# Softmax attention and a slot mixture of experts on one core: late weights, the last values' place, and the merge of the last slots

## The chip, the cores and the metric

The kernel runs on one core of a Trainium2 chip. Its time is the device time of one execution in microseconds (us). Before the change three runs took 321.18, 322.11 and 323.55 us; the median is 322.11.

## The reference

Attention over 8 batches, 12 heads, 448 rows and 64 columns, whose softmax has exp(-m) added to its denominator, and then a mixture of experts with slots: 3584 rows of 768, 32 slots, 8 experts of 4 slots, hidden size 1024.

```python
scores = scale * np.matmul(q, k.transpose(0, 1, 3, 2))
m = np.max(scores, axis=-1, keepdims=True)
e = np.exp(scores - m)
attn = e / (np.sum(e, axis=-1, keepdims=True) + np.exp(-m) + 1e-09)
x = np.matmul(attn, v)                 # laid out as (3584, 768)

logits = x @ phi                       # (3584, 32)
d = np.exp(logits - logits.max(0, keepdims=True))
d /= d.sum(0, keepdims=True) + 1e-09
slot_input = (d.T @ x).reshape(8, 4, 768)
for e in range(8):
    slot_out[e] = np.maximum(slot_input[e] @ w1[e], 0.0) @ w2[e]
c = np.exp(logits - logits.max(1, keepdims=True))
c /= c.sum(1, keepdims=True) + 1e-09
out = c @ slot_out.reshape(32, 768)
```

All inputs and the output are float32; the kernel loads q, k and the weights as bf16 (the DMA converts them) and v as float32.

## The kernel before

**Units and steps.** The attention is cut into 24 units, each of two batches and two heads. A unit has 7 tiles of rows, and the main loop takes one tile per step `n`, so that unit `u` begins at step 7u and the score loop ends at `end` = 168. A plan written by hand, `at(n, where, f)`, sets what else is done at which step and in which place of it: small, av, value, rooms, end, load, in an order that the loop at line 800 shows. Each engine works through its own instructions in the order of the program; nothing is reordered.

**A unit's stages.** `stage_T` transposes q and k on TensorE (L241). `stage_S` forms the scores, and VectorE takes their row maxima (L264). `stage_MT` transposes the maxima (L272), copies them (`mt`, L276) and GpSimd builds from them the matrix `md` (L282, L288). `stage_ST`, ten steps behind the scores, puts -m into PSUM with a matmul by `md` (L300), adds the scores (L305), and ScalarE takes exp (L309). `stage_V` casts v to bf16 on GpSimd (L314). `stage_AV` multiplies (L336), `stage_AVout` copies the product out of PSUM (L347, L350), `stage_den` adds exp(-m) to the sums on GpSimd (L356), and `stage_N` divides (L362, L364). `stage_X` transposes the result for the logits (L419, L420). The last unit, 23, goes another way: `last_sinks` puts exp(-m) in order (L376, L378), and `stage_last` adds, inverts and multiplies straight from PSUM (L387 to L399).

**Mixture.** After every six units, `mixture` forms logits, running maxima and sums, and the slots' input. The last of the four calls does this along `slot_max`, `slot_exp`, `slots_T`, `slot_in` (14 matmuls, L519), `merge` (which weighs the four partial sums by partition block, L626 to L630) and `experts_in`: VectorE adds the new product to the accumulated slots (`ld`, L674), twelve matmuls bring them across partitions (L678), two matmuls give the denominators (L671), and L682, L683 and L685 divide. `gate_logits` in between transposes the logits for the gate (L576). Then come the first expert product (L705), the relu, the second expert product (`outer`, L824) in two halves of columns and two groups of experts, and the output: 28 row tiles, each of two matmuls (L884; the first ones L849 and L881), a copy by VectorE or ScalarE, and a DMA from SyncE's queue (L854, L889).

**Weights.** Each weight load is half an expert matrix: 768 KB as bf16, 1.5 MB in DRAM. 24 of them lie in `wres`, fetched throughout the score loop (L180). The eight others, rooms 0 to 7, are halves of the second matrices of experts 4 to 7. They lie in `block`, where q, k, v, the exponentials and x are until the attention has read them. So their loads come late and in pieces, at the steps that the table at line 789 lists; rooms 6 and 7 follow `slot_in`, which has to read x first. These loads are issued by GpSimd, between its own operations and in order with them; v's loads are issued by SyncE. Each load waits until the former contents of its place have been read.

**Places.** x has seven places in `block`, `x0` and six others in a row; unit u takes place (u + 4) mod 7. The raw values of the last unit lie, before the change, where q and k of that unit were (`qr` and `kr`), which are columns of room 1.

```python
for n, i, js in ((end - 5, 0, (3, 1)), (end - 5, 1, (0, 1)), (end - 2, 1, (1, 3)), (end + 2, 2, (0, 2)),
                 (end + 4, 3, (0, 1)), (end + 4, 2, (2, 2)), (end + 7, 3, (1, 2)), (end + 9, 3, (3, 1)), (end + 9, 4, (0, 3)),
                 (end + 12, 4, (3, 1)), (end + 12, 5, (0, 3)), (end + 18, 5, (3, 1))):
    at(n, "load", lambda i=i, js=js: load_w(WRES + i, *js))
```

Of the kernel before, what the change touches and what calls it, by code (L numbers as in the profile page):

```python
# [20 lines left out]
WRES = 24  # L21
# [3 lines left out]
def kernel(  # L25
# [75 lines left out]
    def xbuf(u):  # L101
        return block[:, ds(xbuf_at((u + 4) % (HP + 1)), N2)]

    def xruns(u):

        runs = []
        for i in range(HP):
            at_ = (u + i + 4) % (HP + 1)
            if runs and at_ > 1 and i % 4:
                runs[-1][1] += 1  # L110
            else:
                runs.append([i, 1, xbuf_at(at_)])
        return [(i, k, block[:, ds(o, k * N2)].rearrange("p (i s n) -> p i s n", i=k, s=TB))
                for i, k, o in runs]
# [40 lines left out]
        RAW[0, "qr"] = t_  # L155

    def load_v(u):
        t_ = block[:, ds(parts["vr" if u < U - 1 else "qr"][0], 2 * N2)].bitcast(F32).rearrange("p (h n) -> p h n", h=2)
        RAW[u, "vr"] = load(u, t_, v, nc.sync if u else nc.gpsimd)

    W = {}
# [5 lines left out]
    def load_w(i, j0=0, m=None, p0=0, rows=128):  # L167


        kind, e, half = weights[i]  # L170
        if kind == 1:
            J, n = KC // 2, F
            src = moe_w1[e].rearrange("(p j) f -> p j f", p=128)[:, ds(half * J, J), :]
        else:
            J, n = FK // 2, DD
            src = moe_w2[e, ds(half * 128 * J, 128 * J)].rearrange("(p j) f -> p j f", p=128)
        js = ds(2 * j0, 2 * (m or J))
        t_ = room(i, n // 2)
        src = src.rearrange("p j (h n) -> p (j h) n", h=2)
        gdma(out=t_[ds(p0, rows), js, :], in_=src[ds(p0, rows), js, :])  # L180
        for j in range(j0, j0 + (m or J)):
            W[kind, e, half * J + j] = t_[:, ds(2 * j, 2), :]
# [187 lines left out]

    def last_sinks(u):
        em = EM.pop(u)
        ems = small.tile([128, 2, TB], F32, tag="den", name="den").rearrange("p b g -> p (b g)")
        DEN[u] = ems
        for b in range(2):
            nc.gpsimd.tensor_copy(  # L376
                ems[:, ts(b, 2 * C3)].rearrange("p (h c) -> p h c", h=2), em[:, :, ds(b * C3, C3)])
        nc.gpsimd.tensor_copy(ems[:, ds(4 * C3, 2)], em[:, :, TB - 1])  # L378

    def stage_last(u):  # L380
        av = AV.pop(u)
        ems = DEN.pop(u)
        drec = small.tile([128, 2, TB], F32, tag="rec", name="rec", bufs=1).rearrange("p b g -> p (b g)")
        x = xbuf(u).rearrange("p (s n) -> p s n", s=TB)
        main = av[:, :, ds(0, 2 * C3 * 65)].rearrange("p b (g e) -> p b g e", e=65)
        rest = av[:, :, ds(2 * C3 * 65, 65)]
        nc.vector.scalar_tensor_tensor(  # L387
            drec[:, ds(0, 4 * C3)].rearrange("p (b g) -> p b g", b=2), main[:, :, :, D], 1e-9,
            ems[:, ds(0, 4 * C3)].rearrange("p (b g) -> p b g", b=2), op0=ALU.add, op1=ALU.add)
        nc.vector.scalar_tensor_tensor(drec[:, ds(4 * C3, 2)], rest[:, :, D], 1e-9,  # L390
                                       ems[:, ds(4 * C3, 2)], op0=ALU.add, op1=ALU.add)
        nc.vector.reciprocal(drec, drec)
        for b in range(2):
            nc.vector.tensor_tensor(
                x[:, ds(b * C3, C3), :].rearrange("p c (h d) -> p h c d", h=2),
                main[:, b].rearrange("p (h c) e -> p h c e", h=2)[:, :, :, ds(0, D)],
                drec[:, ts(b, 2 * C3)].rearrange("p (h c) -> p h c", h=2).unsqueeze(3)
                    .broadcast_to([128, 2, C3, D]), op=ALU.mult)
        nc.vector.tensor_tensor(  # L399
            x[:, TB - 1, :].rearrange("p (h d) -> p h d", h=2), rest[:, :, ds(0, D)],  # L400
            drec[:, ds(4 * C3, 2)].unsqueeze(2).broadcast_to([128, 2, D]), op=ALU.mult)
        X[u] = x


# [27 lines left out]
    def mixture(bp, n, at):  # L432
# [78 lines left out]

        def slot_in():

            ps = slot([128, DD])
            for s, (i, k, x) in ([(s, r) for r in xruns(bp * HP) for s in range(TB)] if final else
                                 [(s, r) for s in range(TB) for r in xruns(bp * HP)]):
                    b, c = divmod(s, C3) if s < 2 * C3 else (0, C3)
                    cs = ds(32 * c, 32)
                    nc.tensor.matmul(ps[cs, ds(i * 128, k * 128)], d_sb[:, b, cs], x[:, :, s, :],  # L519
                                     start=(b == 0 and i % 4 == 0), stop=(b == 1 or c == C3),  # L520
                                     tile_position=(0, 32 * c), skip_group_check=True)
            for i in range(HP):
                X.pop(bp * HP + i)
            if first:
                nc.vector.tensor_copy(acc, ps)
            elif not final:
                rescale(acc, alpha, ps)
            else:
                last_state["ps"] = ps

        if final:
            at(n - 28, "end", lambda: logits((0, 1)))
            at(n - 2, "end", lambda: logits((2, 3, 4), close=False))
            at(n, "end", lambda: logits((5,)))
            at(n, "end", lambda: gate_logits(0))
            at(n, "end", lambda: warm(1))
            at(n + 2, "small", slot_max)
            at(n + 3, "small", slot_exp)
            at(n + 3, "small", lambda: last_state["lT"]())
            at(n + 4, "end", slots_T)  # L540
            at(n + 4, "end", lambda: last_state["gl"][0]())
            at(n + 4, "end", lambda: warm(1))
            at(n, "load", lambda: nc.gpsimd.memset(SI, 0.0))
            at(n + 5, "small", slot_sum)
            at(n + 7, "end", slot_in)
            at(n + 7, "end", lambda: [load_w(WRES + i) for i in (6, 7)])
            at(n + 7, "end", lambda: gate_logits(1))
            at(n + 7, "end", lambda: last_state["gl"][1]())
            at(n + 7, "end", experts_in)
            at(n + 7, "end", experts_hidden)  # L550
        else:
            for j in range(0, HP, 2):
                at(n - 7 * (HP - 2 - j), "end", lambda j=j: logits((j, j + 1)))
# [68 lines left out]
    def merge():  # L622


        for i in range(4):
            nc.vector.tensor_copy(wcol[ds(32 * i, 32), :], ef[:, ds(i, 1)])  # L626
        nc.vector.tensor_scalar(rden, fold, wcol, None, op0=ALU.mult)
# [39 lines left out]

    def experts_in():

        den = slot([128, NS])  # L670
        nc.tensor.matmul(den, sums, rden, start=True, stop=True)  # L671
        si = ld.rearrange("s (p j) -> s j p", j=KC)
        ps = spare(ds(0, KC * NS)).rearrange("p (j n) -> p j n", j=KC)
        nc.vector.scalar_tensor_tensor(ld, acc, last_state["alpha"], last_state["ps"],  # L674
                                       op0=ALU.mult, op1=ALU.add)
        for j in range(KC):
            for i in range(2):
                nc.tensor.matmul(ps[:, j, :], si[:, j, :], fw[:, i, :], start=(i == 0), stop=(i == 1))  # L678
# [68 lines left out]
    def at(n, where, f):  # L747
        plan.setdefault((n, where), []).append(f)

    for u in range(U):  # L750
# [64 lines left out]

    os_ = [slot([128, 384]) for half in range(2)]

    def outer(half, jh, gs):
        J = FK // 2
        for g in gs:  # L820
            for j in range(J):
                for e in range(4):
                    es = ds(32 * e, 32)
                    nc.tensor.matmul(os_[half][es, :], HT[jh][:, g, j, es],  # L824
# [35 lines left out]
    outer(0, 1, (0,))  # L860
    outer(1, 1, (0,))
    first_weights()
    outer(0, 1, (1,))
    nc.scalar.copy(so[:, 0, :], os_[0])
    outer(1, 1, (1,))
    nc.vector.tensor_copy(so[:, 1, :], os_[1])
    first_tiles(0, nc.scalar.copy)
    first_tiles(1, nc.vector.tensor_copy)
# [51 lines left out]
```

## Time and profile before

| | |
|---|---|
| median of three runs | 322.11 us (321.18 to 323.55) |
| profiled execution, own time | 319.92 us |
| its span, first to last instruction | 318.1 us |
| TensorE matmul busy | 277.0 us (87%) |
| VectorE, ScalarE, GpSimd busy | 253.6, 211.7, 229.1 us |
| read from and written to HBM | 83.46 MB, 11.01 MB |
| mean granted TensorE clock | 0.96 |

The profile is of one execution. PE is a matmul on TensorE, PEld a weight load there, DVE is VectorE, ACT ScalarE, POOL GpSimd, SP SyncE. A row of the timeline gives start, duration, engine, line, operation, out<-in, count and, in brackets, how long the engine was idle before it and what ended that. A row of the windows gives for a stretch the busy time of each engine, then the granted TensorE clock, the busy share of the 16 DMA engines and the GB/s that they moved. Where a load converts float32 to bf16, those are the bytes written.

### The profile page before, as it was taken

How to read it: one execution, taken by the hardware profiler on the slowest of the kernel's cores; microseconds unless marked ns; L12 is line 12 of the kernel's file. 1: busy time of each engine (PE TensorE's matmuls, PEld its weight loads, DVE VectorE, ACT ScalarE, POOL GpSimd, SP SyncE). 2: the span in 40 equal slices, each digit the busy share in tenths (PEclk: the TensorE clock that was granted, in tenths of full speed). 3: DMA queues.
4: the chain of work that ended last, by engine and by line, in shares of the span. 5: the costliest groups of instructions: out<-in, count | busy, mean ns of one | idle time of the engine just before them, and what ended most of it. 6: DMA issues, size and time to landing. Idle time of an engine off the chain costs nothing.

```text
span 318.1 us, 13342 instructions
## 1 busy us (share of the span) xinstructions
PE 277.0 (87%) x5861; PEld 159.1 (50%) x5862; DVE 253.6 (80%) x340; ACT 211.7 (67%) x338; POOL 229.1 (72%) x337
## 2 busy tenths in 40 slices
PE   1669989999899899999999999999999988986910
PEld 1325655465555465655655665555556545542300
DVE  2988988898799799999999999999999736527720
ACT  3026867777687677787877788777878885237610
POOL 7476798789898688899898889889984876620000
PEclk9999999999999999999999999999999999998555
DMA  7979999999999979999999999999999799958997
GB/s 131 172 94 187 178 169 190 172 169 183 184 184 192 158 118 174 176 182 145 195 170 184 149 155 202 179 153 154 181 184 195 123 156 202 214 119 305 396 400 287
DMA packets 49130, 59.34 MB, mean 187 GB/s; under 512 B 4560, under 2 KB 44496, under 8 KB 49072
## 3 DMA queue, kind: packets, MB, share of 16 engines
q0 software_dynamic: 37856, 36.46, 76.0%
q1 hardware_dynamic: 11216, 22.03, 20.9%
q8 instruction: 46, 0.75, 0.9%
q14 instruction: 12, 0.10, 0.1%
HBM read 83.46 MB, written 11.01 MB: 297 GB/s over the span
## 4 chain that ended last, share of the span: by engine, by line
PE 67%; DVE 11%; DMA 5%; POOL 5%; issue 4%; ACT 3%; SPq 0%; POOLq 0%; ACTq 0%; DVEq 0%
PE av L336 16%; PE ps L256 12%; PE ps L300 12%; PE ps L305 9%; PE ps L241 6%; DMA block<-in_moe_w_dram 4%; PE ps L419 3%; DVE block L264 3%; PE ps L884 3%; ACT block L309 2%; DVE m L264 2%; PE ps L260 2%; PE av L272 1%; POOL block L282 1%; DMA wres<-in_q_dram 1%
## 5 line engine op out<-in xcount | busy, mean ns | idle before, releaser
L309 ACT ACTIVATE block<-ps 128x896 bf16<-128x896 f32 x168 | 153.8, 917 | 56.0 <-PE ps L305 53.4
L264 DVE TENSOR_REDUCE block<-ps 128x2 bf16<-128x896 f32 x84 | 90.8, 1090 | 15.4 <-PE ps L256 13.8
L264 DVE TENSOR_REDUCE m<-ps 128x2 bf16<-128x896 f32 x84 | 90.8, 1090 | 4.7 <-PE ps L256 3.2
L336 PE MATMUL av<-block 64*128 64x65 bf16 (+1 forms) x2688 | 90.1, 193 | 3.1 <-issue 1.9
L336 PEld LDWEIGHTS <-block 64*128 64x128 bf16 (+1 forms) x2688 | 75.5, 97 | 32.5 <-issue 10.5
L300 PE MATMUL ps<-block,ones 64*64 64x448 bf16 x672 | 69.7, 368 | 4.5 <-POOL block L288 1.4
L305 PE MATMUL ps<-block 64*64 64x448 bf16 x672 | 66.4, 353 | 1.3 <-issue 1.3
L256 PE MATMUL ps<-block 64*128 64x448 bf16 x288 | 54.1, 372 | 3.3 <-DVE m L264 1.3
L256 PEld LDWEIGHTS <-block 64*128 64x128 bf16 x288 | 19.8, 94 | 52.6 <-issue 48.0
L282 POOL TENSOR_TENSOR block<-mt,nmask 128x768 bf16<-128x768 bf16 x24 | 35.2, 1468 | 12.7 <-ACT mt L276 11.6
L136 POOL DMA_DIRECT2D block<-in_q_dram x46 | 27.4, 602 | 18.7 <-PE ps L241 17.3
L364 POOL TENSOR_TENSOR block<-block,rec 128x896 bf16<-128x896 f32 x22 | 37.5, 1704 | 0.5
L180 POOL DMA_DIRECT2D wres<-in_moe_w_dram x48 | 35.0, 731 | 1.4
L300 PEld LDWEIGHTS <-ones 64*64 64x64 bf16 x672 | 24.7, 105 | 9.2 <-issue 4.1
L136 POOL DMA_DIRECT2D block<-in_k_dram x46 | 27.8, 622 | 1.2 <-ACT block L309 1.2
L244 DVE COPY block<-ps 128x896 bf16<-128x896 bf16 x48 | 27.8, 615 | 0.5 <-PE ps L241 0.3
L305 PEld LDWEIGHTS <-block 64*64 64x64 bf16 x672 | 24.5, 107 | 1.8 <-issue 1.7
L241 PE MATMUL ps<-ident,block 128*64 128x128 bf16 x644 | 24.6, 229 | 0.9 <-issue 0.4
L241 PEld LDWEIGHTS <-block 128*64 128x64 bf16 x644 | 20.4, 115 | 4.1 <-issue 2.0
L314 POOL CAST block<-block 128x896 bf16<-128x896 f32 x24 | 22.5, 937 | 0.0
L347 ACT COPY block<-av 128x780 f32<-128x780 f32 x22 | 17.7, 804 | 0.1
L420 DVE COPY block<-ps 128x896 bf16<-128x896 bf16 (+1 forms) x23 | 14.0, 607 | 1.8 <-PE ps L419 1.8
(161 smaller groups left out, 250.3 us busy)
## 6 DMA issues: line engine op xcount, KB each, us to landing
wres<-in_moe_w_dram POOLq DMA_DIRECT2D x48, 384.0 KB, 5.7
out_dram<-wres SPq DMA_DIRECT2D x27, 384.0 KB, 4.5
block<-in_v_dram SPq DMA_DIRECT2D x46, 224.0 KB, 6.2
block<-in_q_dram POOLq DMA_DIRECT2D x46, 112.0 KB, 6.2
block<-in_k_dram POOLq DMA_DIRECT2D x46, 112.0 KB, 6.2
block<-in_moe_w_dram POOLq DMA_DIRECT2D x4, 576.0 KB, 7.6
block<-in_moe_w_dram POOLq DMA_DIRECT2D x2, 768.0 KB, 11.4
block<-in_moe_w_dram POOLq DMA_DIRECT2D x6, 192.0 KB, 6.0
```

The source lines that it names most:

```text
L136: eng.dma_start(out=t_[ds(b * P, P), :, :], in_=src[bp * 2 + b, ds(hp * 2, 2)].rearrange("h (p t) d -> p h (t d)", t=TB))
L180: gdma(out=t_[ds(p0, rows), js, :], in_=src[ds(p0, rows), js, :])
L241: nc.tensor.transpose(ps[ds(h * D, D), :, ds(t * P, P)], r[:, h, ds(t * D, D)], ident)
L244: nc.vector.tensor_copy(t_, ps)
L256: nc.tensor.matmul(ps[:, h, ds(0, S)], QT[u][hs, b, ds(c * 128, 128)], KT[u][hs, b, :], start=True, stop=True)
L264: nc.vector.tensor_reduce(m[:, :, s], ps[:, :, ds(0, S)], axis=AX.X, op=ALU.max)
L282: nc.gpsimd.tensor_tensor(md[:, :, ds(0, C3 * 128)].rearrange("p b (e n) -> p b e n", n=P), mt.unsqueeze(1).unsqueeze(1).broadcast_to([128 ...
L300: nc.tensor.matmul(ps[ds(b * P, P), h, ds(0, S)], ones[hs, :], MD[u][hs, b, :], start=True, stop=False)
L305: nc.tensor.matmul(ps[ds(b * P, P), h, ds(0, S)], KT[u][hs, b, ds(t * P, P)], QT[u][hs, b, :], start=False, stop=True)
L309: nc.scalar.activation(et, ps[:, :, ds(0, S)], AF.Exp, scale=scale)
L336: nc.tensor.matmul(o, et[bs, h, ds(c * 128, w)], V65[u][bs, h, t, ds(0, 65)], start=(t == 0 and h == 0 and c == 0), stop=(t == TB - 1), sk ...
L364: (nc.gpsimd if u < U - 2 else nc.vector).tensor_tensor(x.rearrange("p s (h d) -> p h s d", h=2), xv[:, :, :, ds(0, D)], rec.unsqueeze(3). ...
```

## The change

It has eight parts.

- The raw values of the last unit go to the places of x of units 22 and 23, which are free from the former mixture until those units' x is written.
- The room that this frees in `qr` and `kr` takes two of room 1's four pieces (384 KB), loaded at step `end` - 9; the other two follow at `end` - 5. There is no load at `end` - 2 any more.
- `stage_den` of unit 21 is one step later, so that on GpSimd the last unit's `md` comes ahead of it.
- The load of room 7 is split into a load of three pieces and one of one piece, and the last group of `outer` does the first three pieces for both halves of columns and then the last piece for both. The cast of the first half follows both halves' matmuls in the program.
- `slot_in` of the last mixture writes two tiles of 384 columns in place of one of 768, and `experts_in` merges and multiplies by halves; the denominators' matmuls come between the halves. So that a half of the slots' columns is a set of whole products, the first expert matrix is laid out by contiguous halves.
- `merge` broadcasts the running sum on GpSimd, ahead of its two casts, and no longer on VectorE.
- `stage_last` adds the 14 sums in one instruction; `last_sinks` orders them to fit.
- `xruns` of the last mixture makes runs of three units in place of four and two; the number of matmuls stays 14.

On each engine the order of all other instructions is the same. GpSimd has two instructions more (a load and the broadcast), VectorE one fewer.

```diff
-    def xruns(u):
+    def xruns(u, most=4):
...
-            if runs and at_ > 1 and i % 4:
+            if runs and at_ > 1 and i % most:
...
-        t_ = block[:, ds(parts["vr" if u < U - 1 else "qr"][0], 2 * N2)]...
+        t_ = block[:, ds(parts["vr"][0] if u < U - 1 else xbuf_at((U - 2 + 4) % (HP + 1)), 2 * N2)]...
...
-            src = moe_w1[e].rearrange("(p j) f -> p j f", p=128)[:, ds(half * J, J), :]
+            src = moe_w1[e, ds(half * 128 * J, 128 * J)].rearrange("(p j) f -> p j f", p=128)
...
     def stage_last(u):
...
-        nc.vector.scalar_tensor_tensor(
-            drec[:, ds(0, 4 * C3)].rearrange("p (b g) -> p b g", b=2), main[:, :, :, D], 1e-9,
-            ems[:, ds(0, 4 * C3)].rearrange("p (b g) -> p b g", b=2), op0=ALU.add, op1=ALU.add)
-        nc.vector.scalar_tensor_tensor(drec[:, ds(4 * C3, 2)], rest[:, :, D], 1e-9,
-                                       ems[:, ds(4 * C3, 2)], op0=ALU.add, op1=ALU.add)
+        both = av[:, :, ds(0, TB * 65)].rearrange("p b (g e) -> p b g e", e=65)
+        nc.vector.scalar_tensor_tensor(drec, both[:, :, :, D], 1e-9, ems, op0=ALU.add, op1=ALU.add)
...
-            ps = slot([128, DD])
-            for s, (i, k, x) in ([(s, r) for r in xruns(bp * HP) for s in range(TB)] if final else
+            pss = [slot([128, DD // 2]) for _ in range(2)] if final else [slot([128, DD])]
+            for s, (i, k, x) in ([(s, r) for r in xruns(bp * HP, 3) for s in range(TB)] if final else
                                  [(s, r) for s in range(TB) for r in xruns(bp * HP)]):
+                    ps, i = (pss[i // 3], i % 3) if final else (pss[0], i)
...
-            at(n + 7, "end", lambda: [load_w(WRES + i) for i in (6, 7)])
+            at(n + 7, "end", lambda: [load_w(WRES + 6), load_w(WRES + 7, 0, 3), load_w(WRES + 7, 3, 1)])
...
     def merge():
+        nc.gpsimd.tensor_copy(sums, srun.broadcast_to([128, 128]))
         for i in range(4):
             nc.vector.tensor_copy(wcol[ds(32 * i, 32), :], ef[:, ds(i, 1)])
         nc.vector.tensor_scalar(rden, fold, wcol, None, op0=ALU.mult)
         nc.gpsimd.tensor_copy(fw[:, 0, :], rden)
         nc.gpsimd.tensor_tensor(fw[:, 1, :], rden, fw[:, 0, :], op=ALU.subtract)
-        nc.vector.tensor_copy(sums, srun.broadcast_to([128, 128]))
...
     def experts_in():
-        den = slot([128, NS])
-        nc.tensor.matmul(den, sums, rden, start=True, stop=True)
-        si = ld.rearrange("s (p j) -> s j p", j=KC)
+        si = ld.rearrange("s (a p j) -> s a j p", a=2, j=KC // 2)
         ps = spare(ds(0, KC * NS)).rearrange("p (j n) -> p j n", j=KC)
-        nc.vector.scalar_tensor_tensor(ld, acc, last_state["alpha"], last_state["ps"],
-                                       op0=ALU.mult, op1=ALU.add)
-        for j in range(KC):
-            for i in range(2):
-                nc.tensor.matmul(ps[:, j, :], si[:, j, :], fw[:, i, :], start=(i == 0), stop=(i == 1))
+        for a, half in enumerate(last_state["ps"]):
+            cs = ts(a, DD // 2)
+            nc.vector.scalar_tensor_tensor(ld[:, cs], acc[:, cs], last_state["alpha"], half,
+                                           op0=ALU.mult, op1=ALU.add)
+            for j in range(a * KC // 2, (a + 1) * KC // 2):
+                for i in range(2):
+                    nc.tensor.matmul(ps[:, j, :], si[:, a, j % (KC // 2), :], fw[:, i, :], start=(i == 0), stop=(i == 1))
+            if a == 0:
+                den = slot([128, NS])
+                nc.tensor.matmul(den, sums, rden, start=True, stop=True)
...
-            at(n + 20, "value", lambda u=u: stage_den(u))
+            at(n + (20 if u != U - 3 else 21), "value", lambda u=u: stage_den(u))
...
-    for n, i, js in ((end - 5, 0, (3, 1)), (end - 5, 1, (0, 1)), (end - 2, 1, (1, 3)), (end + 2, 2, (0, 2)),
+    for n, i, js in ((end - 9, 1, (2, 2)), (end - 5, 0, (3, 1)), (end - 5, 1, (0, 2)), (end + 2, 2, (0, 2)),
...
-    def outer(half, jh, gs):
+    def outer(half, jh, gs, js=range(FK // 2)):
...
-            for j in range(J):
+            for j in js:
...
     first_weights()
-    outer(0, 1, (1,))
+    for js in (range(3), (3,)):
+        for half in range(2):
+            outer(half, 1, (1,), js)
     nc.scalar.copy(so[:, 0, :], os_[0])
-    outer(1, 1, (1,))
     nc.vector.tensor_copy(so[:, 1, :], os_[1])
```

More of the change, by code (lines that the diff above doesn't have):

```diff
@@ L157, in load_v @@
     def load_v(u):
-        t_ = block[:, ds(parts["vr" if u < U - 1 else "qr"][0], 2 * N2)].bitcast(F32).rearrange("p (h n) -> p h n", h=2)
+        t_ = block[:, ds(parts["vr"][0] if u < U - 1 else xbuf_at((U - 2 + 4) % (HP + 1)), 2 * N2)].bitcast(F32).rearrange("p (h n) -> p h n", h=2)
         RAW[u, "vr"] = load(u, t_, v, nc.sync if u else nc.gpsimd)
@@ L372, in last_sinks @@
         em = EM.pop(u)
-        ems = small.tile([128, 2, TB], F32, tag="den", name="den").rearrange("p b g -> p (b g)")
+        ems = small.tile([128, 2, TB], F32, tag="den", name="den")
         DEN[u] = ems
@@ L376, in last_sinks @@
             nc.gpsimd.tensor_copy(
-                ems[:, ts(b, 2 * C3)].rearrange("p (h c) -> p h c", h=2), em[:, :, ds(b * C3, C3)])
-        nc.gpsimd.tensor_copy(ems[:, ds(4 * C3, 2)], em[:, :, TB - 1])
+                ems[:, b, ds(0, 2 * C3)].rearrange("p (h c) -> p h c", h=2), em[:, :, ds(b * C3, C3)])
+        nc.gpsimd.tensor_copy(ems[:, :, TB - 1], em[:, :, TB - 1])
     def stage_last(u):
@@ L382, in stage_last @@
         ems = DEN.pop(u)
-        drec = small.tile([128, 2, TB], F32, tag="rec", name="rec", bufs=1).rearrange("p b g -> p (b g)")
+        drec = small.tile([128, 2, TB], F32, tag="rec", name="rec", bufs=1)
         x = xbuf(u).rearrange("p (s n) -> p s n", s=TB)
-        main = av[:, :, ds(0, 2 * C3 * 65)].rearrange("p b (g e) -> p b g e", e=65)
-        rest = av[:, :, ds(2 * C3 * 65, 65)]
-        nc.vector.scalar_tensor_tensor(
-            drec[:, ds(0, 4 * C3)].rearrange("p (b g) -> p b g", b=2), main[:, :, :, D], 1e-9,
-            ems[:, ds(0, 4 * C3)].rearrange("p (b g) -> p b g", b=2), op0=ALU.add, op1=ALU.add)
-        nc.vector.scalar_tensor_tensor(drec[:, ds(4 * C3, 2)], rest[:, :, D], 1e-9,
-                                       ems[:, ds(4 * C3, 2)], op0=ALU.add, op1=ALU.add)
+        both = av[:, :, ds(0, TB * 65)].rearrange("p b (g e) -> p b g e", e=65)
+        nc.vector.scalar_tensor_tensor(drec, both[:, :, :, D], 1e-9, ems, op0=ALU.add, op1=ALU.add)
         nc.vector.reciprocal(drec, drec)
@@ L395, in stage_last @@
                 x[:, ds(b * C3, C3), :].rearrange("p c (h d) -> p h c d", h=2),
-                main[:, b].rearrange("p (h c) e -> p h c e", h=2)[:, :, :, ds(0, D)],
-                drec[:, ts(b, 2 * C3)].rearrange("p (h c) -> p h c", h=2).unsqueeze(3)
+                both[:, b, ds(0, 2 * C3)].rearrange("p (h c) e -> p h c e", h=2)[:, :, :, ds(0, D)],
+                drec[:, b, ds(0, 2 * C3)].rearrange("p (h c) -> p h c", h=2).unsqueeze(3)
                     .broadcast_to([128, 2, C3, D]), op=ALU.mult)
         nc.vector.tensor_tensor(
-            x[:, TB - 1, :].rearrange("p (h d) -> p h d", h=2), rest[:, :, ds(0, D)],
-            drec[:, ds(4 * C3, 2)].unsqueeze(2).broadcast_to([128, 2, D]), op=ALU.mult)
+            x[:, TB - 1, :].rearrange("p (h d) -> p h d", h=2), both[:, :, TB - 1, ds(0, D)],
+            drec[:, :, TB - 1].unsqueeze(2).broadcast_to([128, 2, D]), op=ALU.mult)
         X[u] = x
@@ L524, in slot_in @@
             if first:
-                nc.vector.tensor_copy(acc, ps)
+                nc.vector.tensor_copy(acc, pss[0])
             elif not final:
-                rescale(acc, alpha, ps)
+                rescale(acc, alpha, pss[0])
             else:
-                last_state["ps"] = ps
+                last_state["ps"] = pss
         if final:
```

## Prediction

> **What bounds the kernel now.** I read the page's chain first, then the windows of the last 75 us with their DMA columns, then the timeline of each engine around every edited line. Line numbers are those of the kernel before. The chain in order of time (start, us, what):
>
> ```profile
> 255.70 0.36 POOL block L288
> ...
> 256.11 0.38 PE ps L300 x4
> ...
> 271.52 12.92 DMA block<-in_moe_w_dram
> ...
> 284.48 1.47 PE ps L824 x29
> ...
> 285.98 0.57 DVE wres L866
> ...
> 287.11 0.97 DVE wres L853
> ```
>
> Three things set the end. The last unit's bias matrix on GpSimd lets the scores of L300 start; much later the last weight load lets the last 29 matmuls of L824 start; after them two casts and two copies release the output. The windows say what the DMA engines do meanwhile (last columns: granted clock, DMA share, GB/s written):
>
> ```profile
> 247.00:249.50 2.50, 2.47 (x62) 1.26 (x56) 2.31 (x4) 1.83 (x2) 1.87 (x2) 1.00 0.34 44
> ...
> 258.00:259.60 1.60, 0.85 (x23) 0.40 (x16) 1.26 (x2) 1.60 (x3) 1.43 (x8) 1.00 0.73 90
> 259.60:264.50 4.90, 4.90 (x150) 3.32 (x148) 1.96 (x3) 4.03 (x5) 2.73 (x6) 1.00 1.03 173
> 264.50:283.10 18.60, 16.50 (x275) 9.26 (x274) 10.74 (x38) 6.47 (x17) 10.57 (x14) 1.00 1.05 208
> 283.10:287.20 4.10, 3.08 (x44) 1.61 (x41) 0.65 (x2) 1.92 (x5) 0.00 (x0) 1.00 0.02 3
> ...
> 290.00:316.00 26.00, 11.94 (x44) 3.56 (x41) 11.31 (x12) 9.79 (x14) 0.00 (x0) 0.55 1.01 395
> ```
>
> From 264.5 to 283.1 the late weights stream without a gap at 208 GB/s; then 4 us with nothing to move; then 11 MB of output at 395 GB/s to the end. The output stream is full, so whatever brings its start forward brings the end forward by as much. The tail before that start:
>
> ```profile
> 283.33 0.34 PE L824 MATMUL ps<-block,wres 128*32 128x384 bf16 x3
> ...
> 284.48 1.46 PE L824 MATMUL ps<-block,wres 128*32 128x384 bf16 x29 [0.80 <-DMA block<-in_moe_w_dram]
> ...
> 285.33 0.48 ACT L864 CAST wres<-ps 128x384 bf16<-128x384 f32 x1 [1.29 <-PE ps L824]
> ...
> 286.41 0.86 ACT L853 COPY wres<-ps 128x384 f32<-128x384 f32 x2 [0.60 <-PE ps L849]
> ...
> 286.91 1.58 SPq L854 DMA_DIRECT2D out_dram<-wres  x3
> ...
> 288.12 0.49 PE L832 MATMUL ps<-wres,spread 128*128 128x384 bf16 x2 [0.32 <-DVE wres L853]
> ```
>
> TensorE waits only 0.80 us for the last load. So two chains end nearly together, the loads and TensorE's own work, and a gain on one alone is soon stopped by the other.
>
> **Last values moved, 384 KB fetched early: nothing by itself.** Two pieces of room 1 (384 KB) are now requested nine steps before the end of the score loop, at about 241.4, when the transposes of the last unit have read q and k. The natural hope is that this takes 384 KB off the stream at the end. But each weight load is 786 KB written, and the windows above hold 173 x 4.9 + 208 x 18.6 = 4.72 MB after 259.6, which is six loads exactly: rooms 2 to 7. Rooms 0 and 1 are done by then, and the engines ran short (0.73 and 90 GB/s at 258 to 259.6) before the next request had come. Taking work from ahead of a gap makes the gap longer; the stream behind it starts when its own request is issued. So I price the move at 0 on the stream. The rows that cover its cost:
>
> ```profile
> 240.36 0.98 PE L241 MATMUL ps<-ident,block 128*64 128x128 bf16 x28
> ...
> 244.65 1.47 POOL L282 TENSOR_TENSOR block<-mt,nmask 128x768 bf16<-128x768 bf16 x1 [3.08 <-ACT mt L276]
> ```
>
> ```profile
> block<-in_v_dram SPq DMA_DIRECT2D x4, 224.0 KB, 6.3
> ```
>
> The new request waits on GpSimd for the transposes (to 241.34) and takes 0.5 us; behind it stand the small addition of L356 and L282, and GpSimd is idle 3.08 us before L282 anyway. If that cover went, each microsecond past 244.65 would delay all that follows. The last values' request no longer waits for those transposes, only for an earlier slot product, so SyncE issues it at or before the old 241.5; with 6.3 us to landing it is there by 248, and its cast starts at 252.26 (below). The extra 393 KB written and the values share the queue with what ran before 247, and the window of 247 to 249.5 stands two thirds empty. The other layout of the first expert matrix has the same pieces and bytes; nobody waits for a resident weight in the middle (the only load waited for in the tail is the last one). I take 0 for it too.
>
> **Last maxima first on GpSimd: 0.35 us.** What it removes is a request of 576 KB and a small addition ahead of the bias matrix:
>
> ```profile
> 252.26 0.95 POOL L314 CAST block<-block 128x896 bf16<-128x896 f32 x1
> ...
> 253.51 0.53 POOL L180 DMA_DIRECT2D block<-in_moe_w_dram  x1 [0.30 <-POOL block L314]
> ...
> 254.23 1.47 POOL L282 TENSOR_TENSOR block<-mt,nmask 128x768 bf16<-128x768 bf16 x1
> ...
> 257.65 0.58 POOL L180 DMA_DIRECT2D block<-in_moe_w_dram  x1
> ```
>
> ```profile
> 252.98 0.23 DVE L276 CAST mt<-ps 128x64 bf16<-128x64 f32 x1 [0.46 <-PE ps L272]
> ```
>
> ```profile
> 256.11 0.38 PE L300 MATMUL ps<-block,ones 64*64 64x448 bf16 x4 [0.35 <-POOL block L288]
> ```
>
> GpSimd is free of the cast at 253.21 and the transposed maxima are there at 253.21, so L282 starts at about 253.27 instead of 254.23, 0.96 earlier. TensorE used only 0.35 of that: it waited no longer. So -0.35 on TensorE's chain (bounds 0 and -0.35). On GpSimd the order becomes cast, L282, L288, the addition (0.23), the normalization, and then the request of 257.65: without the 0.30 idle and the 0.53 issue, less some 0.5 in which the normalization must now wait behind the addition and VectorE's reciprocal: -0.35 here as well (bounds 0 and -0.83). That request opens the full stream, and those up to 264.5 hang on the same engines, so the last landing moves from 284.44 to 284.1.
>
> **Merge in halves, one sink addition: 0.4 us on TensorE.** The rows:
>
> ```profile
> 264.69 0.17 DVE L387 SCALAR_TENSOR_TENSOR rec<-av,den 128x12 f32<-128x12 f32 x1 [0.72 <-PE av L336]
> 264.78 0.15 DVE L390 SCALAR_TENSOR_TENSOR rec<-av,den 128x2 f32<-128x2 f32 x1
> ```
>
> ```profile
> 269.50 0.84 PE L519 MATMUL ps<-block,d_sb 128*32 128x512 bf16 x14 [0.30 <-ACT d_sb L510]
> ...
> 269.89 0.24 DVE L627 TENSOR_SCALAR rden<-fold,wcol 128x32 f32<-128x32 bf16 x1
> ...
> 270.26 0.66 PE L576 MATMUL ps<-ident,lTs 128*128 128x128 f32 x4
> ...
> 270.38 1.01 DVE L674 SCALAR_TENSOR_TENSOR ld<-acc,al,ps 128x768 bf16<-128x768 f32 x1
> ...
> 270.75 0.31 PE L671 MATMUL ps<-rden,block 128*128 128x32 f32 x2
> ...
> 271.46 0.73 PE L678 MATMUL av<-fw,ld 128*128 128x32 bf16 x12 [0.40 <-DVE ld L674]
> ...
> 271.53 0.35 DVE L683 RECIPROCAL rden<-rden 128x32 f32<-128x32 f32 x1
> ...
> 272.29 0.42 DVE L685 TENSOR_TENSOR block<-av,rden 128x96 bf16<-128x96 f32 x2 [0.40 <-PE av L678]
> ```
>
> One addition in place of two overlapping ones saves the 0.09 between their starts (bounds 0 and -0.15). The 14 slot matmuls keep their columns, so their first half is there at 269.92; VectorE is free at 270.13, since the broadcast of the sum now runs on GpSimd beside it. Two merges of about 0.51 (half of 1.01) then end at 270.66 and 271.17. TensorE leaves the four transposes at 270.9, does six of the L678 matmuls (0.36), the moved denominator (0.31) and the other six, done near 271.7 instead of 272.19. Then VectorE is last: the denominator ends at about 271.45, the addition takes 0.18 and the reciprocal 0.35, so L685 starts near 272.0 instead of 272.29. That is -0.3. Bounds: -0.5 (TensorE's own gain) and +0.3 (the moved denominator's 0.31 wholly on the way). GpSimd's casts, which need the result of L627, stand behind the broadcast there, which can run from 269.3, before it. TensorE's chain sums to 0.35 + 0.09 + 0.30 = 0.74, and it is busy without a wait from there to L824: it reaches the last group at 282.6.
>
> **Last piece in two parts: most of the gain.** Of the last 768 KB, three quarters are one request and 192 KB the next, at 284.1 - 0.94 = 283.15 (197 KB at 208 GB/s) and 284.1. The last group now does 24 matmuls of both halves on the first and 8 on the second. By 1.46 / 29 = 0.05 us each the 24 need 1.2, from 282.6 with a wait to 283.15 after the first three: done at 284.2. The 8 need 0.4: both sums are there near 284.6 instead of 285.95. The first half's sum, which ScalarE had at 285.33, comes after four of the eight: 284.55, so the first two output requests (192 KB each) come 0.8 earlier. The second half's copy, until now at 287.11, waits for both casts and TensorE's two small products and starts near 285.9: 1.2 earlier. L832, and so every tile from the fifth, hangs on that copy. The stream is full only after these tiles, so I take 1.2 for the whole. Bounds: if the landing doesn't move, 0.4 after 284.44 gives 284.9 and the outputs gain 0.5 to 0.85; if landing stops mattering, TensorE's 282.6 + 32 x 0.05 = 284.2 gives 1.75.
>
> A row against the split: with little queued ahead, a weight load took 3.5 us at the least from issue to landing:
>
> ```profile
> DMA to landing us min/median/max: 3.5/5.5/7.0
> ```
>
> That is its price if it ran after the other, but the stream above shows loads of 192 KB queued among others at 208 GB/s with no such gaps. The Trainium skill ("DMA: Bandwidth & Descriptors", section "Anatomy of one DMA — SWDGE (gpsimd) path") gives a fixed 2.0 us and bytes / 436 GB/s for each. For 393 KB read that would be an estimated 2.9 us in series, an end 0.55 us later than now; laid over one another, as the trace has them, the fixed part falls once.
>
> **Sum.** The profiled execution took 319.92, 1.82 outside its span of 318.1. Less 1.2: 318.7. It stands 2.19 below the median of the runs, 322.11; the same 1.2 off the median gives **320.9 us** (0.37%).
>
> **Rivals.**
> First, the 384 KB do come off the stream at the end: 393 KB at 208 GB/s are 1.9 us, landing near 282.2, and TensorE becomes the bound at 284.2. Gain 1.75, 320.4. For it speaks the stream's length; against it the gap at 258 and the count of six loads. Chance 0.12.
> Second, the order on GpSimd doesn't help, because the request of 257.65 stays where it was behind the later normalization, and TensorE meets another wait at 256.11. Landing stays at 284.44; only the split remains, 0.8: 321.3. Against it: the maxima are there when the cast ends. Chance 0.20.
> Third, slower: the last 192 KB start only when the load before has landed. 283.15 + 3.5 = 286.65, plus 0.45 gives 287.1 against 285.95: +1.15, 323.3. It decides as soon as the last part lands more than 1.9 us after the first part (then 8 matmuls end past 285.5, and the late casts of both halves at once eat the rest). Against it the unbroken stream. Chance 0.10.
>
> **How the numbers follow.** The forecast has 0.58. The runs shown spread from 321.18 to 323.55, and a difference of about 1% (3.2 us) is what a measurement of this kernel can tell from no change. No case reaches that by its own sum; with the runs' spread and what I haven't seen, faster by over 1% (below 318.9) gets 0.12, from the forecast and the first rival; slower by over 1% gets 0.08, from the third; 0.80 stays within. The range runs from 319.0 (the first rival less 1.4 of spread) to 323.3 (the third).
>
> **What would show it.** L282 of the last unit about 1 us earlier against the cast before it; no wait at its L300; a wider gap in the DMA columns near 255 to 259 and the stream after it as long as now; the last group in 24 and 8 matmuls with a wait of under 1 us ahead of each; the first output request 0.8 and the second half's copy 1.2 us earlier against the start. I am wrong if the stream shortens by over 1 us, if the last part lands over 1.5 us after the first, or if a cast of values or the resident weights wait for a load.

## The result, and the profile after

| | before | after |
|---|---|---|
| median of 22 runs each | 323.34 us (321.15 to 325.61) | 320.57 us (317.49 to 323.78) |
| ratio after / before | | 0.9911, 95% interval 0.9886 to 0.9937 |
| profiled execution, its span | 319.92, 318.1 us | 320.78, 319.0 us |

A ratio leaves out the runs that are more than 1.5% above the fastest of the same kernel; the medians and ranges count every run.

The kernel became 2.9 us faster (2.0 to 3.7). The predicted time of 320.9 holds, but in part by luck: the predicted gain was 1.2, which is 1.7 too small, and it was taken off the median of three runs, 322.11, which lies 1.2 below that of the 22.

The two profiled executions can't be compared as wholes: that of before was shorter than every one of its 22 timed runs. Apart from the moved loads both run the same instructions up to the last unit, yet they reach its cast of the maxima (L276) at 252.98 and 254.02 us. So the tail is read from that cast on, as a mark: it lasts 65.12 us before and 64.98 after in these two. The timeline of after (its lines are some five lower from `stage_last` on):

```profile
253.28 0.95 POOL L314 CAST block<-block 128x896 bf16<-128x896 f32 x1
...
254.02 0.22 DVE L276 CAST mt<-ps 128x64 bf16<-128x64 f32 x1 [0.46 <-PE ps L272]
...
254.33 1.47 POOL L282 TENSOR_TENSOR block<-mt,nmask 128x768 bf16<-128x768 bf16 x1
...
256.69 1.69 POOL L364 TENSOR_TENSOR block<-block,rec 128x896 bf16<-128x896 f32 x1 [0.35 <-DVE rec L362]
...
258.32 0.58 POOL L180 DMA_DIRECT2D block<-in_moe_w_dram  x1
```

The bias matrix (L282) follows the cast at once, and the request of room 2 comes 4.30 us after the mark instead of 4.67. The windows after (last columns: clock, DMA share, GB/s):

```profile
257.00:259.00 2.00, 2.00 (x60) 1.19 (x56) 0.36 (x1) 2.00 (x4) 2.00 (x3) 1.00 0.12 22
259.00:261.00 2.00, 1.25 (x42) 0.59 (x36) 0.91 (x2) 1.72 (x3) 1.83 (x8) 1.00 0.75 94
...
265.00:283.50 18.50, 16.60 (x278) 9.13 (x277) 10.69 (x37) 6.54 (x17) 11.34 (x17) 1.00 1.07 206
```

The gap ahead of the stream has grown. The engines' share is 0.12 at 257 to 259, which is 3 to 5 us after the mark. Before had 0.96 from 4 to 5 us after its mark, the row below, and 0.73 in the 1.6 us behind that:

```profile
257.00:258.00 1.00, 1.00 (x34) 0.56 (x37) 0.00 (x0) 1.00 (x2) 1.00 (x2) 1.00 0.96 194
```

The stream behind the gap runs as long as before at the same rate. The tail after the change:

```profile
283.61 0.34 PE L823 MATMUL ps<-block,wres 128*32 128x384 bf16 x3
...
285.06 1.46 PE L823 MATMUL ps<-block,wres 128*32 128x384 bf16 x29 [1.12 <-DMA block<-in_moe_w_dram]
...
286.40 0.48 ACT L865 CAST wres<-ps 128x384 bf16<-128x384 f32 x1 [2.10 <-PE ps L823]
...
287.78 0.96 DVE L852 COPY wres<-ps 128x768 f32<-128x768 f32 x1 [0.66 <-PE ps L848]
287.96 1.32 SPq L853 DMA_DIRECT2D out_dram<-wres  x3
```

The last two requests, issued at 271.95 and 272.49, took 13.1 and 13.5 us to land:

```profile
DMA to landing us min/median/max: 13.1/13.3/13.5
```

So three quarters of room 7 are there at 285.02 and the last 192 KB at 285.99. TensorE begins on the first and doesn't wait for the second here: 29 matmuls without a stop, done 0.53 after the last landing, where before they began with it and took 1.46. (In a third trace of the changed kernel, n3_after, the two landings lie 1.40 us apart, and it waits 0.25 for the second.)

### The profile page after: what moved, and what is told of

Same layout as the page of the kernel before. It is cut to its first block, busy times and chain, and to the rows that moved or that the text cites. A ratio compares the mean times of both kernels' runs of the same rounds, so it can differ in the third digit from the quotient of the medians.

```text
span 319.0 us, 13352 instructions
## 1 busy us (share of the span) xinstructions
PE 277.6 (87%) x5862; PEld 159.3 (50%) x5862; DVE 253.7 (80%) x339; ACT 211.7 (66%) x338; POOL 230.2 (72%) x339
## 4 chain that ended last, share of the span: by engine, by line
PE 70%; DVE 12%; DMA 6%; ACT 4%; issue 3%; POOL 1%; SPq 0%; ACTq 0%; DVEq 0%; POOLq 0%
PE av L336 17%; PE ps L256 13%; PE ps L300 12%; PE ps L305 10%; PE ps L241 6%; DMA block<-in_moe_w_dram 4%; DVE block L264 4%; PE ps L414 3%; PE ps L884 3%; DVE m L264 2%; ACT block L309 2%; PE ps L260 2%; DMA wres<-in_q_dram 1%; PE av L272 1%; DVE wres L888 1%
## 5 line engine op out<-in xcount | busy, mean ns | idle before, releaser
L264 DVE TENSOR_REDUCE block<-ps 128x2 bf16<-128x896 f32 x84 | 90.8, 1090 | 14.9 <-PE ps L256 13.1
L282 POOL TENSOR_TENSOR block<-mt,nmask 128x768 bf16<-128x768 bf16 x24 | 35.3, 1470 | 12.1 <-ACT mt L276 10.9
L347 ACT COPY block<-av 128x780 f32<-128x780 f32 x22 | 17.7, 804 | 0.4 <-PE av L336 0.4
L888 DVE COPY wres<-ps 128x768 f32<-128x768 f32 x13 | 12.2, 957 | 3.9 <-PE ps L884 3.6
```

The lines of the kernel that those rows point to most:

```text
L264: nc.vector.tensor_reduce(m[:, :, s], ps[:, :, ds(0, S)], axis=AX.X, op=ALU.max)
L282: nc.gpsimd.tensor_tensor(md[:, :, ds(0, C3 * 128)].rearrange("p b (e n) -> p b e n", n=P), mt.unsqueeze(1).unsqueeze(1).broadcast_to([128 ...
```

## The experiments

The question was why the runs gained 2.9 us and the tail's parts only some 1. My theory, called the sum theory in the expectations, was the prediction's: split, order on GpSimd and merge, nothing from the layout or from the 384 KB. The rivals: the layout of the first expert matrix, the stream relieved of 384 KB, and a gain that only both chains together give. Twelve runs in three groups, each group on one chip and beside its own runs of the kernel before. The marks are from each trace, in us after the cast of the last maxima: "last sink sum" is the start of VectorE's addition to the last unit's sums (L387 before), "slots divided" the start of the division of the slots' input (L685 before), "last landing" that of the last weights, and "end" the end of the span:

| run | what it has | ratio (95%) | last sink sum | slots divided | last landing | end |
|---|---|---|---|---|---|---|
| before | | | 11.71 | 19.31 | 31.5 | 65.12 |
| n1_before | | 0.998 (0.995 to 1.002) | 11.73 | 19.32 | 32.2 | 65.98 |
| e1_layout | layout | 0.999 (0.996 to 1.003) | 11.73 | 19.07 | 31.7 | 65.45 |
| e1b | layout | 0.996 (0.992 to 1.000) | 11.72 | 19.07 | 32.3 | 65.95 |
| e8_merge | layout, merge | 0.998 (0.994 to 1.002) | 11.72 | 19.08 | 32.3 | 66.08 |
| e9_early_split_den | early, split, order | 1.000 (0.997 to 1.003) | 11.18 | 18.77 | 32.4 | 65.52 |
| e9b | early, split, order | 0.997 (0.993 to 1.000) | 11.17 | 18.76 | 31.9 | 65.77 |
| e5_no_split | all but the split | 0.987 (0.983 to 0.992) | 11.18 | 18.53 | 32.3 | 66.80 |
| e6_no_early | all but the early load | 0.993 (0.990 to 0.996) | 11.71 | 19.06 | 32.3 | 65.69 |
| e7_no_den | all but the order | 0.986 (0.981 to 0.990) | 11.18 | 18.53 | 31.4 | 64.78 |
| e11_no_merge | all but the merge | 0.990 (0.986 to 0.994) | 11.18 | 18.52 | 31.7 | 64.47 |
| after | all | 0.991 (0.989 to 0.994) | 11.18 | 18.53 | 32.0 | 64.98 |
| n2_after | all | 0.989 (0.983 to 0.994) | 11.17 | 18.52 | 31.5 | 64.90 |
| n3_after | all | 0.993 (0.990 to 0.996) | 11.17 | 18.53 | 31.5 | 64.55 |

The marks of TensorE's and VectorE's chain repeat within 0.02 us; the landing spreads by 1 us, and the end with it.

**The kernel before, unchanged (n1_before).**

> The kernel before, unchanged, for a second profile and for the spread. Every theory: ratio 1.00 within its interval. The profiled execution of before was 319.9 us, below the 22 runs of before (321.2 to 325.6). If that execution was a lucky one, this one is 1 to 4 us longer, and the place where it is longer shows what the median of before contains: in the score loop before 250 us, or in the stream of late weights, whose end would then come later than 31.5 us after the cast of the last maxima.

Its execution took 323.16 us: 2.44 us more than the first one up to the mark, 0.86 more behind it. The first trace was a short one in both stretches.

**The layout alone (e1_layout, e1b).**

```diff
-            src = moe_w1[e].rearrange("(p j) f -> p j f", p=128)[:, ds(half * J, J), :]
+            src = moe_w1[e, ds(half * 128 * J, 128 * J)].rearrange("(p j) f -> p j f", p=128)
...
-        si = ld.rearrange("s (p j) -> s j p", j=KC)
+        si = ld.rearrange("s (a p j) -> s a j p", a=2, j=KC // 2)
...
-                nc.tensor.matmul(ps[:, j, :], si[:, j, :], fw[:, i, :], start=(i == 0), stop=(i == 1))
+                nc.tensor.matmul(ps[:, j, :], si[:, j // (KC // 2), j % (KC // 2), :], fw[:, i, :], start=(i == 0), stop=(i == 1))
```

> Only the other layout of the first expert matrix (contiguous halves), with the slots' columns read to match. My theory (nobody waits for resident weights): ratio 1.000, within 0.003. Rival, the layout: contiguous halves load faster and ease the queue that q, k and v share, and this is the surplus of the measured 2.9 us over my 1.2: ratio 0.993 to 0.996.

> The layout alone a second time, on the same chip. Layout in the loop: ratio 0.992 to 0.996, and the cast of the last maxima 1 to 2 us earlier on the whole than in kernels with the old layout. Sum theory: 0.998 to 1.000; the division of the slots' input 0.25 us earlier against the cast of the maxima, since the twelve weight loads read the merged slots at half the stride, and nothing of that at the end.

**Layout and merge (e8_merge), and all but the merge (e11_no_merge).** The first takes the split, the early load and the order out of the changed kernel; the second puts the parts below back into it, and with them the slots' input in one tile, the two sink additions and the runs of four and two.

```diff
-        for a, half in enumerate(last_state["ps"]):
+        nc.vector.scalar_tensor_tensor(ld, acc, last_state["alpha"], last_state["ps"], op0=ALU.mult, op1=ALU.add)
...
-        nc.gpsimd.tensor_copy(sums, srun.broadcast_to([128, 128]))
+        nc.vector.tensor_copy(sums, srun.broadcast_to([128, 128]))
```

> The layout, the slots' input and the merge in halves, the broadcast on GpSimd and the single sink addition, without the early 384 KB, the order on GpSimd and the split of the last piece. My theory: TensorE's chain 0.4 us shorter, but the last landing is unchanged, so at most 0.1 us of it reaches the end: ratio 0.999 to 1.000. Layout rival: 0.993 to 0.996, as the layout alone.

> The changed kernel with one merge over all columns, the broadcast on VectorE and two sink additions, as before. If the halves are worth nothing: ratio equal to the changed kernel of this call within 0.002, and the division of the slots' input 18.5 to 18.6 us after the cast of the maxima, as there. If the halves carry the 0.25 us: 18.8.

The merge in halves, the broadcast on GpSimd and the single sink addition are worth nothing on this chain: with them and without them the slots are divided at 19.08 and 19.07, and at 18.53 and 18.52. What I had credited to them comes from the layout. TensorE's twelve small matmuls in the layout alone, and in e9b with the old one:

```profile
271.44 0.49 PE L678 MATMUL av<-fw,ld 128*128 128x32 bf16 x12 [0.40 <-DVE ld L674]
```

```profile
273.56 0.73 PE L678 MATMUL av<-fw,ld 128*128 128x32 bf16 x12 [0.39 <-DVE ld L674]
```

Each loads 128 columns of the merged slots, at a stride of three elements instead of six; 0.49 against 0.73 is the 0.25 us.

**Early load, split and order without layout and merge (e9_early_split_den, e9b).** The kernel before with the diff's lines for these three.

> The last values' place with the early 384 KB, the order on GpSimd and the split of the last piece, without the layout and the merge in halves. My theory: nearly the whole gain, 1.0 to 1.2 us by the prediction's sum: ratio 0.996 to 0.997. Rival, the stream: in most executions the queue does not run dry at 258 us, the 384 KB come off its end, and this gives 2 to 2.9 us: 0.991 to 0.994. Layout rival: 0.997 to 1.000.

> Early load, order on GpSimd and split without layout and merge, a second time, on the same chip as the changed kernel. Sum theory: within 0.001 of the changed kernel (TensorE's 0.25 us from the layout is all that is missing, and it does not reach the end while the landing is later). Layout in the loop: 0.004 to 0.008 above the changed kernel. Trace by every theory: last additions 0.5 us earlier against the cast of the maxima, as before.

These two ratios are 1.000 and 0.997, those of the layout alone 0.999 and 0.996. Each is too wide to tell 0.3% from nothing, so I put the runs together, every timed run of each group:

| all timed runs | old layout | new layout |
|---|---|---|
| without early load, split, order | 323.2 (120 runs: before, n1) | 322.0 (35: e1 twice, e8) |
| with them | 321.4 (24: e9 twice) | 320.3 (40: the changed kernel three times) |

Against 323.2 the medians differ by -1.15 (95% interval -2.0 to -0.3) for the layout, -1.75 (-2.1 to -0.4) for the three others and -2.9 (-3.4 to -2.25) for all; the first two add up to the third. Means give -1.2, -1.3 and -2.8; with only the runs that the ratios use the medians give -1.0 (-1.9 to -0.1), -1.3 (-1.9 to 0.0) and -2.5 (-3.2 to -1.9). So the layout is worth about as much as the rest, but only the pool tells: on the first chip the two kernels with the layout and without the three others have medians of 322.2, and the second set of runs of the kernel before (n1) has 322.0. Nor do the traces show it: the cast of the last maxima comes at 254.5 us on the mean of the four traces with the old layout and at 254.2 in the ten with the new, where e1b's expectation was 1 to 2 us. The rival "both chains together" isn't needed, though the intervals leave room for 1 us of it.

**The whole again, and without one part each.**

> The changed kernel again, beside the others of this call. What is open: 0.991 for the whole, but 1.000 and 0.998 for its two halves, and in the traces the changed kernel's output ends 33.0 us after the last landing instead of 33.7. Theory of the sum (split 0.7, GpSimd's order and TensorE's chain 0.4): ratio 0.996 to 0.997. Rival, the two chains together: only with both shortened does the end move, and the whole gains more than its halves: 0.990 to 0.993 again.

> The changed kernel a third time, on the same chip as the next three. In the traces so far the stretch from the cast of the last maxima to the end is 64.8 to 65.0 us in the changed kernel and 65.1 to 66.1 in kernels without the early load and the split; that is some 0.7 us, while the medians differ by 2.8. Either the rest lies ahead of that cast, where only the layout of the first expert matrix differs, or it is spread of the runs. Sum theory: ratio 0.996 to 0.998. Repeat of what was measured: 0.988 to 0.992.

The repeats lie at 0.989 and 0.993; the first result was no accident.

> The changed kernel with the last load whole and the last group in the old order. Sum theory: the last 29 matmuls wait for the whole load, the output ends 33.7 us after the landing again, 0.7 us later than in the changed kernel: ratio 0.998 to 0.999, and 0.002 above the changed kernel. Rival: the split is worth nothing, equal to the changed kernel.

```diff
-            at(n + 7, "end", lambda: [load_w(WRES + 6), load_w(WRES + 7, 0, 3), load_w(WRES + 7, 3, 1)])
+            at(n + 7, "end", lambda: [load_w(WRES + i) for i in (6, 7)])
...
-    for js in (range(3), (3,)):
-        for half in range(2):
-            outer(half, 1, (1,), js)
+    outer(0, 1, (1,))
     nc.scalar.copy(so[:, 0, :], os_[0])
+    outer(1, 1, (1,))
```

By its runs it can't be told from the changed kernel (0.987 and 0.989 on that chip). By the traces the end follows the last landing by 33.7 us in the five kernels with a whole load beside this one (33.66 to 33.80), and by 33.3 on average in the eight with a split one (32.8 to 33.9). In this one it is 34.5; its wait was longer and the clock fell:

```profile
284.00 1.57 PE L823 MATMUL ps<-block,wres 128*32 128x384 bf16 x29 [2.38 <-DMA block<-in_moe_w_dram]
```

```profile
284.00:286.50 2.50, 2.50 (x33) 1.21 (x33) 0.56 (x1) 0.61 (x2) 0.00 (x0) 0.74 0.00 0
```

> The changed kernel with the last values in the old place and room 1's pieces at the old steps, so that the request of 576 KB again stands ahead of the last bias matrix on GpSimd. My theory: the move is worth nothing to the stream (it opens with the request of room 2) but its place on GpSimd is worth up to 0.35 us: ratio at most 0.002 above the changed kernel. Stream rival: 0.004 to 0.006 above it, and the last landing 1 to 2 us later after the cast of the maxima.

```diff
-        t_ = block[:, ds(parts["vr"][0] if u < U - 1 else xbuf_at((U - 2 + 4) % (HP + 1)), 2 * N2)]...
+        t_ = block[:, ds(parts["vr" if u < U - 1 else "qr"][0], 2 * N2)]...
...
-    for n, i, js in ((end - 9, 1, (2, 2)), (end - 5, 0, (3, 1)), (end - 5, 1, (0, 2)), ...
+    for n, i, js in ((end - 5, 0, (3, 1)), (end - 5, 1, (0, 1)), (end - 2, 1, (1, 3)), ...
```

GpSimd and TensorE there:

```profile
253.60 0.95 POOL L314 CAST block<-block 128x896 bf16<-128x896 f32 x1
254.85 0.53 POOL L180 DMA_DIRECT2D block<-in_moe_w_dram  x1 [0.30 <-POOL block L314]
255.39 1.48 POOL L282 TENSOR_TENSOR block<-mt,nmask 128x768 bf16<-128x768 bf16 x1
```

```profile
257.27 0.38 PE L300 MATMUL ps<-block,ones 64*64 64x448 bf16 x4 [0.18 <-POOL block L288]
```

The order alone does nothing on TensorE's chain: the request of 576 KB still stands between the cast and the bias matrix, and the last sink sum stays at 11.71. The landing, 32.3, is 0.7 later than in the three traces of the changed kernel on average, which is within its spread and about a third of the 1.9 us of the stream rival.

The windows go against that rival too. In the eight traces with the early load the engines' share falls to 0.02 to 0.17 from 4 to 5 us after the mark; in the six without it the lowest, from 5 to 6 us after it, is 0.44 to 0.77. So the 384 KB were carried where the gap now is.

The runs, however, say more than the traces. On its chip this kernel's median is 321.6 (12 runs) against 319.4 of the changed kernel (6): 2.2 us more (95% interval 0.0 to 3.4). The ratios differ by 0.0044, which is what the stream rival expected (0.004 to 0.006) and not my at most 0.002. Against the changed kernel's 40 runs on all chips it is 1.3 us (0.1 to 1.9). So the early load is probably worth more than its place on GpSimd, and no trace shows where.

> The changed kernel with the small addition of unit 21 at its old step, ahead of the last bias matrix on GpSimd. With the request gone from there, the bias matrix starts only 0.2 us later, which TensorE's wait of 0.35 us before hid in part: ratio equal to the changed kernel within 0.001. Rival, that order is the step that counts: 0.002 or more above it.

```diff
-            at(n + (20 if u != U - 3 else 21), "value", lambda u=u: stage_den(u))
+            at(n + 20, "value", lambda u=u: stage_den(u))
```

```profile
255.78 0.95 POOL L314 CAST block<-block 128x896 bf16<-128x896 f32 x1
256.67 0.23 POOL L356 TENSOR_TENSOR den<-block,em 128x14 f32<-128x14 f32 x1
256.85 1.47 POOL L282 TENSOR_TENSOR block<-mt,nmask 128x768 bf16<-128x768 bf16 x1
```

Here the addition is back ahead of the bias matrix, and the last sink sum is at 11.18 as in the changed kernel. So the whole gain at this place comes from the request that went, none from the order. The order even has a price on GpSimd: room 2 is requested 3.75 us after the mark here and 4.30 after it in the changed kernel. Neither the landing (31.4) nor the ratio (0.986 against 0.989) tells it from noise.

**What the layout does to the loads.** The page's line of GpSimd's DMA queue (packets, MB, share of the 16 engines' time), with the old layout (e9b) and with the new one (n3_after), on one chip and with the same number of packets:

```profile
q0 software_dynamic: 38000, 36.46, 76.2%
```

```profile
q0 software_dynamic: 38000, 36.46, 75.2%
```

From the packets' records in each trace: the 12,288 packets of 1,024 bytes, which are the first expert matrix and nothing else, took 113 to 116 ns each (mean 115.1) in the four traces with the old layout and 108 to 113 (mean 110.5) in the ten with the new; packets of 896 bytes (q and k) took 90 to 91 in all. These packets take some 4% less where the rows of one load lie in one block of DRAM. How that shortens the kernel the traces don't show. A candidate is TensorE's wait for k and q of a coming unit, such as this one (n2_after):

```profile
87.49 0.58 PE L241 MATMUL ps<-ident,block 128*64 128x128 bf16 x14 [0.53 <-DMA block<-in_k_dram]
```

From 20 to 250 us such waits sum to 0.3 to 1.6 us in eleven of the fourteen traces and to 0.1 or nothing in before, e8 and after. But they aren't shorter with the new layout (0.8 on the mean of ten traces) than with the old (0.6 of four). And single executions of the same loop reach the mark between 251.7 and 256.5 us, which hides 1 us.

## Why the prediction was right, and where not

- **The layout of the first matrix, priced at 0: wrong.** It is the term that fails: 1.15 us (0.3 to 2.0) by the pooled runs. I argued that nobody waits for a resident weight. But the same engines move q, k and v and the late weights, and before's window over the loop has them at a share of 1.00; I asked who waits for the load and not what else uses the engine. That this is the way the gain comes about is argued, not shown. The layout also gave TensorE's 0.25 us, which I hadn't seen.

```profile
20.00:250.00 230.00, 221.24 (x5061) 130.89 (x5060) 209.06 (x257) 175.32 (x273) 194.50 (x278) 1.00 1.00 170
```

- **The 384 KB, 0 on the stream: right as far as the traces go.** The gap grew and the stream stayed. With the request of room 2 earlier by 0.37 (predicted 0.35), the last landing is on average 31.8 in the eight traces without the 576 KB request and 32.0 in the six with it: 0.2 of 0.35, not told from 0 with a spread of 1. As a price of the whole move it is doubtful: by the runs of e6 the move is worth 2.2 us (0.0 to 3.4), and my sum has 0.35 for it.
- **Last maxima first: right place, one of its two causes, and too small a bound.** 0.54 us on TensorE's chain instead of 0.35. TensorE's rows showed one wait of 0.35, and I took it for the most that could be gained. I named the request and the addition together; the removed request brings all of it.
- **Merge in halves and one sink addition, -0.39: wrong**, 0.00 to 0.01 each. With the halves the moved denominators end 17.7 us after the mark, and VectorE's addition to them starts at 17.82; with one merge (e11) it starts at 17.80. The forecast's own rows also add up to less: 270.92 + 0.36 + 0.31 + 0.36 is 271.95, not 271.7, and by the same steps the division gains 0.17, not 0.30. TensorE's sum of 0.74 came out at 0.76 only because the layout's 0.25 and the larger 0.54 took the place.
- **Split: right in kind.** In after, the parts land 0.97 apart (0.94 predicted; 0.40 to 1.40 in the eight traces with a split load), the last group ends 0.53 after the last landing (0.45), the first output request comes 0.5 earlier against the landing (0.45; the same in five of the eight traces, and 0.2 or less in three), the second half's copy 0.9 (0.85). The end gains 0.5 of that, not 0.85. The Trainium skill ("DMA: Bandwidth & Descriptors", "Anatomy of one DMA — SWDGE (gpsimd) path") gives each such DMA a fixed 2.0 us; 0.97 between the two landings shows that behind this backlog it isn't paid twice.
- **The rivals.** The last part landing late: refuted by the two landings. The stream relieved of 384 KB: against it stand the windows and the landings, for it the runs of e6, whose gain has no place in the traces. The order that doesn't help is what e6 and e7 show, but the request's removal did.
- **The tail in sum:** from the mark to the end 64.81 in three traces of the changed kernel, 65.72 in five without early load and split: 0.9 for 1.2 predicted, nearer than its terms deserved.

What stays open: how the faster packets reach the end, what the early load saves beyond its place on GpSimd, and whether the two halves of the change only add.

## What to carry to other kernels

Where the DMA engines are busy all the time, a load's access pattern can have a price even if its data is needed much later; ask what else moves on the same engines. Taking bytes from ahead of a gap in a stream left the stream's end where it was here, but taking their request out of GpSimd's queue brought TensorE's chain 0.54 us forward. And where single executions differ by 1%, compare stretches from a common mark inside the trace before you compare spans.

## What the runs showed of the hardware that I had not expected

Twelve weight loads on TensorE with the columns at a stride of three instead of six elements let their matmuls run in 0.49 us instead of 0.73. Where a load reads one contiguous 768 KB block of DRAM instead of every other 12 KB of twice the range, its packets took 4% less time (110.5 against 115.1 ns). After 2.38 us without a matmul TensorE's granted clock fell to 0.50 for 3.4 us in e5 (0.74 on the mean of the 2.5 us shown). The length of the wait alone doesn't tell when that happens: in the loop the clock fell to 0.50 within 2 us of waits of 1.90 us (e7) and 1.52 us (e11), and it stayed at 1.00 after waits of 1.85 us (e1b) and 1.89 us (e8).
